# A Fourier filter with a gated convolution: the remainder of the gated input on GpSimd instead of VectorE for nine of the last ten blocks

## The chip, the cores and the metric

The kernel runs on one core of one Trainium2 chip. The metric is the device time of one execution in microseconds (us), lower is better. The core has TensorE (PE in the profile, its weight loads are PEld), VectorE (DVE), ScalarE (ACT), GpSimd (POOL) and the queue of SyncE (SP), which issues nearly all DMAs here. The engines run side by side and each works through its own instructions in order.

## The reference

```python
def _attn_ref(x, w_r, w_i, b_r, b_i):          # x: (8, 3200, 256)
    X = np.fft.rfft(x, axis=1)
    Yr = Xr @ w_r - Xi @ w_i + b_r
    Yi = Xr @ w_i + Xi @ w_r + b_i
    # soft threshold of both parts by 0.01
    y = np.fft.irfft(Yr + 1j * Yi, n=3200, axis=1)

def _moe_ref(x, w_val, conv_w, w_out):         # x is y from above
    gate_pre = sum(conv_w[k] * xp[:, k:k + S, :] for k in range(5))   # causal, per channel
    gate = 1 / (1 + np.exp(-gate_pre))
    val = x @ w_val
    return (gate * val) @ w_out                # (8, 3200, 256)
```

So each of eight batches goes through a Fourier transform, a complex channel mixing with a threshold, the inverse transform, and then a gated block: a causal convolution with five taps and a sigmoid make the gate, a 256x256 product makes the value, and the gated value is multiplied by `w_out`.

## The kernel before, in words

The transform is split into two factors (64 and 50) so that TensorE can do it with small matrices, with two passages through DRAM for each batch. The gated part of a batch is done in eight blocks of 400 positions, written (b, k) below for batch b and block k. All 64 blocks but the last, (7,7), go through the same steps:

- **positions** (L779): 128 small matmuls finish the inverse transform into `y_p` (L803), and ScalarE copies the block into `y_sb` (L810).
- **taps** (L844): for two blocks at once (for the last two blocks, (7,6) and (7,7), one at a time) ScalarE computes the first tap of each of two channel halves into an accumulator `acc` (L857), VectorE adds the other four taps, eight instructions in all (L860, called *tap steps* below, 800 elements in each partition for a pair, 400 for a single block), and ScalarE applies the sigmoid (L871).
- **value**: TensorE multiplies the block by `w_val` into `v_ps`. From block (6,7) on this is done with plain fp32 weights (L831, 4 matmuls, which the profile counts as 8), before that with high and low parts (L835, 12 matmuls).
- **product** (L902): VectorE multiplies `v_ps` in PSUM with the sigmoid in `acc` and writes the gated value back to `acc`.
- **split** (L353): ScalarE rounds the gated value to a high part (L360, the *cast*), and VectorE subtracts it from the gated value, which gives the low part (L362, the *remainder*). Both lie in `gated`.
- **output**: TensorE multiplies `gated` by the high and low parts of `w_out` into `o_ps` (L835, 12 matmuls), ScalarE copies it to `o` (L926), and SP stores it (L928). The last block (7,7) has no split: its gated value is multiplied in plain fp32 (L831).

The order of the work is made before the program is built. Every piece of work is entered into a plan with its engine, a due time, a duration in a table of costs (`dve`, `act` and the like) and the pieces it needs. `Plan.order` (L115) then goes through the plan as a list scheduler: at each step it takes the engine whose next piece can begin first, and among the pieces that can begin within a slack of that time the one that is due first. The instructions are written in that order, so each engine's queue is fixed. The buffers rotate with fixed numbers of slots: `v_ps`, `o_ps` and `y_p` share two PSUM slots (`ps_2`), `acc` has two, `gated` has two (`g_hl`) and `o` has two. The first writer of a slot waits for all readers of the tile that had it before.

GpSimd has only a few memsets at the start and two additions (L937) which make the plain fp32 weights.

The two lines that the change touches are the remainder in `split` and its call in `gated`:

```python
add(at + 0.001, "DVE", dve(n), lambda: nc.vector.tensor_tensor(out=low(), in0=src(),
    in1=f32(high()), op=ALU.subtract), [*uses, hl[0]], [hl[1]])
gs = [*split(at + own("gate", b) + 0.1, 2 * TB, kh, gate, ...
```

Of the kernel before, what the change touches and what calls it, by code (L numbers as in the profile page):

```python
# [11 lines left out]
F32R = mybir.dt.float32r  # L12
# [3 lines left out]
ALU = mybir.AluOpType  # L16

B, S, D = 8, 3200, 256
P = 128
# [9 lines left out]
TB = NH * MB * N2  # L29
# [54 lines left out]
class Plan:  # L84
# [11 lines left out]
    def add(self, at, engine, busy, fn, uses=(), sets=(), new=None, delay=None, mode="r", kb=0, chain=None, extra=0, moves=1, ways=16, ins=0):  # L96
        n = len(self.pieces)
        before = set()
        for key in uses:
            before |= set(self.writers.get(key, ()))  # L100
        for key in sets:
            before |= set(self.readers.get(key, ())) | set(self.writers.get(key, ()))
        for key in uses:
            self.readers.setdefault(key, []).append(n)
        for key in sets:
            self.writers[key], self.readers[key] = [n], []
        p = dict(n=n, at=round(at, 5), engine=engine, busy=busy, fn=fn, before=before, new=new or {}, mode=mode, kb=kb, extra=extra, moves=moves, ways=ways, ins=ins,
                 tiles={key[:2] for key in (*uses, *sets)}, delay=busy + LAND[engine] if delay is None else delay)
        p["behind"] = {self.last[chain]} if chain in self.last else set()
        if chain:  # L110
            self.last[chain] = n
        self.pieces.append(p)
        return n
# [132 lines left out]
def dve(n, copy=False):  # L246
    return 67 + n / (1.92 if copy else 0.96)


def act(n, kind="copy"):  # L250
    return {"copy": 45, "cast": 95, "mul": 104, "conv": 187, "relu": 198, "sigmoid": 103}[kind] + n / 1.2
# [42 lines left out]
         "acc": 2, "g_hl": 2, "o": 2, "ps_s2": 2, "ps_y": 1, "ps_k": 2, "ps_2": 2, "a_dram": 2, "z_dram": 2}  # L294


LATE = [(b, k) for b in (B - 2, B - 1) for k in range(NB)]


@with_exitstack  # L300
def fourier_filter_then_gated_conv(ctx: ExitStack, tc: tile.TileContext, x, w_r, w_i, b_r, b_i,
                                   w_val, conv_w, w_out, f1, f2, g1, g2, eye, out):
    nc = tc.nc
# [3 lines left out]
    dram = ctx.enter_context(tc.tile_pool(name="dram", bufs=2, space=bass.MemoryType.DRAM))  # L307
    LATE_VAL, LATE_OUT = set(LATE[int(O["late_val"]):]), set(LATE[int(O["late_out"]):])
    plan = Plan(SLOTS)
    add = plan.add  # L310
    tl = {}

    def f32(ap):
        return ap.bitcast(F32)
# [20 lines left out]
    def buffer(key, tag, shape, dtype=F32):  # L335
        if tag == "ps_k":
            tl[key] = k_bank[:, k_count[0] % 2, :]
            k_count[0] += 1
            return tl[key]
        pool = ps if tag.startswith("ps_") else dram if tag.endswith("_dram") else sb  # L340
        tl[key] = pool.tile(shape, dtype, name=key[0], tag=tag, bufs=SLOTS[tag])
        return tl[key]
# [7 lines left out]
    def two_banks(key):  # L350
        return buffer(key, "ps_2", [P, 2, 512])

    def split(at, n, key, src, high, low, uses=(), new=None, first=None):  # L353

        hl = key + ("high",), key + ("low",)

        def cast():
            if first:
                first()
            nc.scalar.copy(out=high(), in_=src())  # L360
        add(at, "ACT", act(n, "cast"), cast, uses, [hl[0]], new, chain=key[0])
        add(at + 0.001, "DVE", dve(n), lambda: nc.vector.tensor_tensor(out=low(), in0=src(), in1=f32(high()), op=ALU.subtract),  # L362
            [*uses, hl[0]], [hl[1]])
        return hl

# [409 lines left out]
    def y_at(k, c, tap=H0):  # L775
        lo = (k * MB + tap) * N2
        return y_sb[:, c, :, lo:lo + MB * N2]
# [48 lines left out]
    def matrix(key, e, w, src, whole):  # L826
        p = two_banks(key) if e == 0 else tl[key]
        n = 0
        if whole:
            for c in range(2):  # L830
                nc.tensor.matmul(p[:, e, 0:TB], w()[:, c, e * P:(e + 1) * P], src(0, c), start=c == 0, stop=c == 1)  # L831
            return
        for c in range(2):
            for hw, hy in ((0, 0), (1, 0), (0, 1)):
                nc.tensor.matmul(p[:, e, 0:TB], w[:, hw, c, e * P:(e + 1) * P], src(hy, c), start=n == 0, stop=n == 5)  # L835
                n += 1

    def blocks_at_once(b, k):
        return 1 if b == B - 1 and k >= NB - 2 else 2

    def own(name, b):
        return O[name] + O.get(f"{name}_{b}", 0.0)
# [31 lines left out]
    def gated(b, k, at):  # L874
        bk = (b, k)
        here = [("y", k, 0)]
        nb = blocks_at_once(b, k)
        k0 = k - k % nb
        ky, kv, kh, kp, ko = (("y_hl", bk), ("v_ps", bk), ("gated", bk), ("o_ps", bk), ("o", bk))
        if bk in LATE_VAL:  # L880
            vs = [*here, ("w_late", 0, 0)]
            vm = lambda e: matrix(kv, e, lambda: w_late[0], lambda h, c: y_at(k, c), True)
        else:
            src = y_sb[:, :, :, (k * MB + H0) * N2:(k * MB + H0 + MB) * N2]
            view = lambda j: tl[ky][:, j].rearrange("p c (h n) -> p c h n", h=NH)
            vs = [*split(at + own("y", b), 2 * TB, ky, lambda: src, lambda: view(0), lambda: view(1), here, {ky: "y_hl"},
                         lambda: buffer(ky, "y_hl", [P, 2, 2, TB], F32R)), ("w", "w_val", "high"), ("w", "w_val", "low")]
            vm = lambda e: matrix(kv, e, wv_sb, lambda h, c: tl[ky][:, h, c, :], False)
        if k == k0:

            vs = [*vs, *[("y", j, 0) for j in range(k + 1, k + nb)]]
        for e in range(2):
            add(at + own("val", b), "PE", 1344 if bk in LATE_VAL else 1092, lambda e=e: vm(e), vs, [kv + (e,), *([("turn", "read", (b, 2 + e))] if k == NB - 1 else [])],
                {kv: "ps_2"} if e == 0 else None, chain="val", ins=12)


        kg = ("acc", (b, k0))
        gate = lambda: tl[kg][:, :, :, (k - k0) * MB * N2:(k - k0 + 1) * MB * N2]
        hn = lambda ap: ap.rearrange("p c (h n) -> p c h n", h=NH)
        if k == k0:  # L900
            taps(b, k0, nb, at)
        add(at + own("gate", b), "DVE", dve(2 * TB), lambda: nc.vector.tensor_tensor(  # L902
            out=gate(), in0=hn(tl[kv][:, :, 0:TB]), in1=gate(), op=ALU.mult), [kv + (0,), kv + (1,), kg + (0,), kg + (1,)], [kg + ("gated", k)])
        if bk in LATE_OUT:
            gs = [kg + ("gated", k), ("w_late", 0, 0)]
            om = lambda e: matrix(kp, e, lambda: w_late[1], lambda h, c: gate()[:, c], True)
        else:
            gs = [*split(at + own("gate", b) + 0.1, 2 * TB, kh, gate, lambda: hn(tl[kh][:, 0]), lambda: hn(tl[kh][:, 1]),
                         [kg + ("gated", k)], {kh: "g_hl"}, lambda: buffer(kh, "g_hl", [P, 2, 2, TB], F32R)),
                  ("w", "w_out", "high"), ("w", "w_out", "low")]  # L910
            om = lambda e: matrix(kp, e, wo_sb, lambda h, c: tl[kh][:, h, c, :], False)
        for e in range(2):
            add(at + own("project", b), "PE", 1344 if bk in LATE_OUT else 1092, lambda e=e: om(e), gs, [kp + (e,)],
                {kp: "ps_2"} if e == 0 else None, ins=12)
        dst = out[b].rearrange("(c p) n -> p c n", p=P)[:, :, k * TB:(k + 1) * TB]
        kind = at + own("project", b) + 0.1
        if bk == (B - 1, NB - 1):
            def keep(e):
                o = buffer(ko, "o", [P, 2, TB]) if e == 0 else tl[ko]
                (nc.scalar.copy, nc.vector.tensor_copy)[e](out=o[:, e], in_=tl[kp][:, e, 0:TB])  # L920
            for e, eng in enumerate(("ACT", "DVE")):
                add(kind, eng, act(TB) if e == 0 else dve(TB), lambda e=e: keep(e), [kp + (e,)], [ko + (e,)],
                    {ko: "o"} if e == 0 else None)
                add(kind, "SP", 400, lambda e=e: nc.sync.dma_start(out=dst[:, e], in_=tl[ko][:, e]), [ko + (e,)], (), kb=200)
            return
        add(kind, "ACT", act(2 * TB), lambda: nc.scalar.copy(out=buffer(ko, "o", [P, 2, TB]), in_=tl[kp][:, :, 0:TB]),  # L926
            [kp + (0,), kp + (1,)], [ko + (0,)], {ko: "o"})
        add(kind, "SP", 400, lambda: nc.sync.dma_start(out=dst, in_=tl[ko]), [ko + (0,)], (), kb=400)  # L928
# [102 lines left out]
```

## Time and profile before

| what | value |
|---|---|
| time, median of 3 runs | 879.93 us (878.89 to 881.42) |
| profiled execution, its own time | 881.59 us |
| span of the profiled execution | 879.8 us, granted TensorE clock 0.994 on average |
| busy: PE, DVE, ACT, POOL | 857.8, 759.1, 604.9, 3.8 us |
| remainders of the gated input (L362, `gated`), from 690 us on | 21, together 20.6 us |
| tap steps of the last batch begin | 823.90 us |
| last product ends | 872.63 us (starts at 871.64, takes 0.99) |
| last block's output product on PE | starts at 872.91 us |

A row of the timeline gives the start, the time it took, the engine, the line, the operation and the tiles written and read, with their partitions and elements; in brackets stands how long the engine was idle before it, and what ended the idle time. Consecutive instructions of one engine overlap a little in the profile, so the time that one takes out of an engine is the distance of two starts. In groups and sources, three numbers with slashes are the shortest, median and longest duration in ns.

### The profile page before, as it was taken

How to read it: one execution, taken by the hardware profiler on the slowest of the kernel's cores; microseconds unless marked ns; L12 is line 12 of the kernel's file. 1: busy time of each engine (PE TensorE's matmuls, PEld its weight loads, DVE VectorE, ACT ScalarE, POOL GpSimd, SP SyncE). 2: the span in 40 equal slices, each digit the busy share in tenths (PEclk: the TensorE clock that was granted, in tenths of full speed). 3: DMA queues.
4: the chain of work that ended last, by engine and by line, in shares of the span. 5: the costliest groups of instructions: out<-in, count | busy, mean ns of one | idle time of the engine just before them, and what ended most of it. 6: DMA issues, size and time to landing. Idle time of an engine off the chain costs nothing.

```text
span 879.8 us, 24544 instructions
## 1 busy us (share of the span) xinstructions
PE 857.8 (97%) x10400; PEld 745.5 (85%) x10400; DVE 759.1 (86%) x1143; ACT 604.9 (69%) x928; POOL 3.8 (0%) x11
## 2 busy tenths in 40 slices
PE   7999999999999999999999999999999999998997
PEld 3778788878999898898899889898899999998775
DVE  2346888999989996999879997899969999899796
ACT  2456666977677766877667776877658775875664
POOL 0000000000000000000000000000100000000000
PEclk9999999999999999999999999999999999999999
DMA  6878886786554476565855576646746353423522
GB/s 212 253 244 253 240 269 197 265 251 199 165 184 146 148 218 212 177 185 172 272 168 171 175 237 205 218 122 208 244 133 202 104 171 94 142 103 110 186 76 94
DMA packets 105289, 163.34 MB, mean 186 GB/s; under 512 B 9690, under 2 KB 78172, under 8 KB 105180
## 3 DMA queue, kind: packets, MB, share of 16 engines
q1 hardware_dynamic: 103764, 158.43, 58.1%
q10 hardware_dynamic: 1416, 3.34, 1.2%
q8 instruction: 82, 1.34, 0.6%
q14 instruction: 27, 0.22, 0.1%
HBM read 82.05 MB, written 79.69 MB: 184 GB/s over the span
## 4 chain that ended last, share of the span: by engine, by line
PE 78%; DVE 15%; DMA 3%; ACT 2%; issue 1%; SPq 0%; ACTq 0%; DVEq 0%
PE y_ps L704 14%; PE o_ps L835 12%; PE v_ps L835 11%; PE s L634 9%; PE z_ps L747 8%; PE k_bank L709 7%; PE y_p L803 6%; DVE acc L860 6%; PE p L583 5%; DMA x<-in_x 2%; PE warm L951 1%; DVE acc L902 1%; PE v_ps L831 1%; DMA f_sb<-in_f 1%; DVE gated L362 1%
## 5 line engine op out<-in xcount | busy, mean ns | idle before, releaser
L860 DVE SCALAR_TENSOR_TENSOR acc<-y_sb,cw_sb,acc 128x800 f32<-128x800 f32 (+1 forms) x264 | 258.7, 1017 | 11.4 <-ACT acc L857 11.2
L704 PE MATMUL y_ps<-w_sb,xs 128*128 128x256 f32 x1152 | 157.7, 286 | 0.7 <-DVE yb L718 0.7
L835 PE MATMUL o_ps<-gated,wo_sb 128*128 128x400 f32 x756 | 153.5, 352 | 0.0
L704 PEld LDWEIGHTS y_ps<-w_sb,xs 128*128 128x128 f32 x1152 | 144.3, 190 | 8.6 <-issue 3.9
L835 PEld LDWEIGHTS o_ps<-gated,wo_sb 128*128 128x128 f32 x756 | 135.6, 189 | 3.4 <-issue 1.0
L835 PE MATMUL v_ps<-y_hl,wv_sb 128*128 128x400 f32 x660 | 130.6, 346 | 1.1 <-ACT y_sb L810 1.1
L634 PEld LDWEIGHTS s<-f_sb,a 128*128 128x128 f32 x800 | 100.3, 191 | 24.9 <-issue 19.0
L835 PEld LDWEIGHTS v_ps<-y_hl,wv_sb 128*128 128x128 f32 x660 | 118.7, 188 | 2.1 <-ACT y_sb L810 1.3
L634 PE MATMUL s<-f_sb,a 128*128 128x128 f32 x800 | 111.9, 280 | 1.3 <-DVE xs L692 1.2
L747 PE MATMUL z_ps<-tp,g_sb 64*64 64x256 f32 x1536 | 93.7, 380 | 0.0
L688 ACT CAST xs<-s 128x512 fp32r<-128x512 f32 x96 | 56.2, 586 | 43.0 <-PE y_ps L704 28.1
L709 PE MATMUL k_bank<-w_sb,xs 128*128 128x256 f32 x576 | 85.3, 283 | 0.4 <-DVE yb L715 0.4
L722 ACT ACTIVATE tp<-yb,nlam 128x512 f32<-128x512 f32 (+1 forms) x104 | 73.6, 708 | 16.5 <-DVE yb L718 9.0
L718 DVE TENSOR_TENSOR yb<-y_ps,yb 128x512 f32<-128x512 f32 x96 | 65.4, 681 | 19.9 <-PE y_ps L704 19.7
L747 PEld LDWEIGHTS z_ps<-tp,g_sb 64*64 64x64 f32 x1536 | 57.1, 133 | 27.1 <-issue 5.8
L360 ACT CAST gated<-acc 128x800 fp32r<-128x800 f32 x63 | 54.2, 861 | 37.1 <-DVE acc L902 33.5
L709 PEld LDWEIGHTS k_bank<-w_sb,xs 128*128 128x128 f32 x576 | 74.8, 188 | 5.1 <-issue 1.1
L926 ACT COPY o<-o_ps 128x800 f32<-128x800 f32 x63 | 51.9, 823 | 38.0 <-PE o_ps L835 37.8
L803 PEld LDWEIGHTS y_p<-g_sb,zl 50*64 50x64 f32 x4096 | 66.1, 135 | 13.9 <-issue 5.1
L902 DVE TENSOR_TENSOR acc<-v_ps,acc 128x800 f32<-128x800 f32 x64 | 62.9, 983 | 16.9 <-PE v_ps L835 14.1
L724 DVE SCALAR_TENSOR_TENSOR tp<-yb,tp 128x512 f32<-128x512 f32 (+1 forms) x104 | 68.8, 661 | 7.7 <-ACT tp L722 7.4
L803 PE MATMUL y_p<-g_sb,zl 50*64 50x50 f32 x4096 | 71.8, 220 | 3.4 <-issue 2.2
(80 smaller groups left out, 1028.4 us busy)
## 6 DMA issues: line engine op xcount, KB each, us to landing
zl<-z_dram SPq DMA_DIRECT2D x128, 200.0 KB
out<-o SPq DMA_DIRECT2D x63, 400.0 KB
a_dram<-s SPq DMA_DIRECT2D x120, 208.0 KB
a<-a_dram SPq DMA_DIRECT2D x96, 256.0 KB
z_dram<-z_t SPq DMA_DIRECT2D x48, 512.0 KB
x<-in_x SPq DMA_DIRECT2D x120, 200.0 KB
a_dram<-s ACTq DMA_DIRECT2D x8, 208.0 KB
x<-in_x ACTq DMA_DIRECT2D x8, 200.0 KB
```

The source lines that it names most:

```text
L634: nc.tensor.matmul(spec()[:, c, :, i, :], tl[ka][:, i0 + i, c * P:(c + 1) * P], f2_of(i), start=True, stop=True)
L688: nc.scalar.copy(out=tl[kx][:, 0:512], in_=tl[k2].rearrange("p a b -> p (a b)"))
L704: nc.tensor.matmul(p[:, 1 - r, :], xm(hx, c, r), w_sb[:, m, hw, c, :], start=k == 0, stop=k == 5)
L709: nc.tensor.matmul(p, sm(hx, c), w_sb[:, 0, hw, c, :], start=k == 0, stop=k == 5)
L718: add(at + 0.2, "DVE", dve(2 * D), lambda: nc.vector.tensor_tensor(out=yb(), in0=tl[ky], in1=yb(), op=ALU.add), [ky + (0,)], [kb + (0,)])
L722: nc.scalar.activation(out=buffer(kt, "tp", [P, 2, D])[:, 0:n], in_=tl[kb][:, 0:n], func=AF.Relu, bias=nlam)
L724: add(at + 0.2, "DVE", dve(n * D), lambda: nc.vector.scalar_tensor_tensor(out=tl[kt][:, 0:n], in0=tl[kb][:, 0:n], scalar=LAM, in1=tl[kt][: ...
L747: nc.tensor.matmul(p[e * HP:(e + 1) * HP, i, j * D:(j + 1) * D], g[i * HP:(i + 1) * HP, r, e * HP:(e + 1) * HP], tl[kts[j]][i * HP:(i + 1) ...
L803: nc.tensor.matmul(pv[h][e * HP:(e + 1) * HP, c, m, :], zt[half(h), m, c * P + e * HP:c * P + (e + 1) * HP], g2_sb[half(h), :], start=True ...
L835: nc.tensor.matmul(p[:, e, 0:TB], w[:, hw, c, e * P:(e + 1) * P], src(hy, c), start=n == 0, stop=n == 5)
L860: nc.vector.scalar_tensor_tensor(out=acc(c), in0=y_of(c, j), scalar=cw_sb[:, c, j:j + 1], in1=acc(c), op0=ALU.mult, op1=ALU.add)
L902: add(at + own("gate", b), "DVE", dve(2 * TB), lambda: nc.vector.tensor_tensor(out=gate(), in0=hn(tl[kv][:, :, 0:TB]), in1=gate(), op=ALU. ...
```

## The change

The remainder (the subtraction that gives the low part) is issued on GpSimd for blocks (6,6), (6,7) and (7,0) to (7,6). The last block, (7,7), has no remainder. In the plan it is entered for engine POOL with a cost of 2.7 ns for each of 800 elements instead of `dve(800)`. Operands and tiles are the same. The 54 earlier remainders of the gated input stay on VectorE, and so do all those of `y_hl`.

```diff
+POOL_LOW = 2.7
 LATE = [(b, k) for b in (B - 2, B - 1) for k in range(NB)]
...
-    def split(at, n, key, src, high, low, uses=(), new=None, first=None):
+    def split(at, n, key, src, high, low, uses=(), new=None, first=None, pool=False):
...
         add(at, "ACT", act(n, "cast"), cast, uses, [hl[0]], new, chain=key[0])
-        add(at + 0.001, "DVE", dve(n), lambda: nc.vector.tensor_tensor(out=low(), in0=src(), in1=f32(high()), op=ALU.subtract),
+        eng, busy = ("POOL", POOL_LOW * n) if pool else ("DVE", dve(n))
+        add(at + 0.001, eng, busy, lambda: (nc.gpsimd if pool else nc.vector).tensor_tensor(out=low(), in0=src(), in1=f32(high()), op=ALU.subtract),
             [*uses, hl[0]], [hl[1]])
...
             gs = [*split(at + own("gate", b) + 0.1, 2 * TB, kh, gate, lambda: hn(tl[kh][:, 0]), lambda: hn(tl[kh][:, 1]),
-                         [kg + ("gated", k)], {kh: "g_hl"}, lambda: buffer(kh, "g_hl", [P, 2, 2, TB], F32R)),
+                         [kg + ("gated", k)], {kh: "g_hl"}, lambda: buffer(kh, "g_hl", [P, 2, 2, TB], F32R), pool=bk >= (B - 2, 6)),
```

Since the plan is made with the new engine and cost, the order of other pieces changes too, but only from the product of block (6,7) on; ahead of it every engine's queue is as before. Up to the first function the line numbers of the changed kernel are 1 higher, behind `split` 2 higher: the tap steps are L862 there, the products L904, the remainder L364, the value and output products L833 and L837.

The first place is VectorE in the middle of the last batch, from the first tap step of that batch. `acc_10622` is the accumulator of blocks (7,0) and (7,1); `acc_10745` before and `acc_10740` now is that of (7,2) and (7,3); `acc_10879` before and `acc_10907` now is that of (7,4) and (7,5). Before:

```order
L860 SCALAR_TENSOR_TENSOR acc_10622<-y_sb_78,cw_sb_76,acc_10622 128x800 x8
L362 TENSOR_TENSOR gated_10639<-acc_10359,gated_10639 128x800
L902 TENSOR_TENSOR acc_10622<-v_ps_10727,acc_10622 128x4x200
L860 SCALAR_TENSOR_TENSOR acc_10745<-y_sb_78,cw_sb_76,acc_10745 128x800
L902 TENSOR_TENSOR acc_10622<-v_ps_10740,acc_10622 128x4x200
L362 TENSOR_TENSOR gated_10759<-acc_10622,gated_10759 128x800
L860 SCALAR_TENSOR_TENSOR acc_10745<-y_sb_78,cw_sb_76,acc_10745 128x800
L362 TENSOR_TENSOR gated_10803<-acc_10622,gated_10803 128x800
L860 SCALAR_TENSOR_TENSOR acc_10745<-y_sb_78,cw_sb_76,acc_10745 128x800 x6
L860 SCALAR_TENSOR_TENSOR acc_10879<-y_sb_78,cw_sb_76,acc_10879 128x800 x2
L902 TENSOR_TENSOR acc_10745<-v_ps_10899,acc_10745 128x4x200
```

Now:

```order
L862 SCALAR_TENSOR_TENSOR acc_10622<-y_sb_78,cw_sb_76,acc_10622 128x800 x8
L862 SCALAR_TENSOR_TENSOR acc_10740<-y_sb_78,cw_sb_76,acc_10740 128x800 x3
L904 TENSOR_TENSOR acc_10622<-v_ps_10751,acc_10622 128x4x200
L862 SCALAR_TENSOR_TENSOR acc_10740<-y_sb_78,cw_sb_76,acc_10740 128x800 x5
L904 TENSOR_TENSOR acc_10622<-v_ps_10872,acc_10622 128x4x200
L904 TENSOR_TENSOR acc_10740<-v_ps_10899,acc_10740 128x4x200
L862 SCALAR_TENSOR_TENSOR acc_10907<-y_sb_78,cw_sb_76,acc_10907 128x800 x5
L904 TENSOR_TENSOR acc_10740<-v_ps_10928,acc_10740 128x4x200
L862 SCALAR_TENSOR_TENSOR acc_10907<-y_sb_78,cw_sb_76,acc_10907 128x800 x3
L904 TENSOR_TENSOR acc_10907<-v_ps_10957,acc_10907 128x4x200
```

The remainders are gone from VectorE's queue, the tap steps of (7,2) and (7,3) have moved ahead of the products of (7,0) and (7,1), and the products of (7,1) and (7,2) now stand next to each other, where eleven instructions lay between them before.

The second place is TensorE at the same point, in the changed kernel: `v_ps_10872`, `v_ps_10899` and `v_ps_10928` are the values of (7,1), (7,2) and (7,3), and the `o_ps` rows are the outputs of (7,0) and (7,1).

```order
L833 MATMUL v_ps_10872<-y_sb_78,w_late_8659 128x400 x4
L837 MATMUL o_ps_10882<-gated_10833,wo_sb_74 128x400 x12
L833 MATMUL v_ps_10899<-y_sb_78,w_late_8659 128x400 x4
L837 MATMUL o_ps_10909<-gated_10896,wo_sb_74 128x400 x12
L833 MATMUL v_ps_10928<-y_sb_78,w_late_8659 128x400 x4
```

The three tiles `v_ps_10872`, `o_ps_10882` and `v_ps_10899` are taken in this order from the two slots of `ps_2`, so the third has the slot of the first. Before, the values of (7,0) and (7,1) stood together ahead of the output of (6,7).

The third place is GpSimd behind the two additions, in the changed kernel (before, nothing stands there): the nine remainders in the order of the blocks.

```order
L364 TENSOR_TENSOR gated_10498<-acc_10359,gated_10498 128x800
L364 TENSOR_TENSOR gated_10639<-acc_10359,gated_10639 128x800
L364 TENSOR_TENSOR gated_10833<-acc_10622,gated_10833 128x800
L364 TENSOR_TENSOR gated_10896<-acc_10622,gated_10896 128x800
L364 TENSOR_TENSOR gated_10925<-acc_10740,gated_10925 128x800
L364 TENSOR_TENSOR gated_10955<-acc_10740,gated_10955 128x800
L364 TENSOR_TENSOR gated_10980<-acc_10907,gated_10980 128x800
L364 TENSOR_TENSOR gated_11004<-acc_10907,gated_11004 128x800
L364 TENSOR_TENSOR gated_11043<-acc_10973,gated_11043 128x800
```

The last place is VectorE's end, in the changed kernel: `acc_10907` is the pair (7,4), (7,5), `acc_10973` is block (7,6) and `acc_11025` is block (7,7).

```order
L904 TENSOR_TENSOR acc_10907<-v_ps_10957,acc_10907 128x4x200
L862 SCALAR_TENSOR_TENSOR acc_10973<-y_sb_78,cw_sb_76,acc_10973 128x400 x2
L904 TENSOR_TENSOR acc_10907<-v_ps_10969,acc_10907 128x4x200
L862 SCALAR_TENSOR_TENSOR acc_10973<-y_sb_78,cw_sb_76,acc_10973 128x400 x6
L904 TENSOR_TENSOR acc_10973<-v_ps_11000,acc_10973 128x800
L862 SCALAR_TENSOR_TENSOR acc_11025<-y_sb_78,cw_sb_76,acc_11025 128x400 x8
L904 TENSOR_TENSOR acc_11025<-v_ps_11059,acc_11025 128x800
L922 COPY o_11093<-o_ps_11085 128x400
```

Before, the same tap steps and products stood here with four remainders between them. The order of the stores on SP is unchanged.

## The prediction

> **What bounds the kernel now.** First the page: TensorE is busy nearly throughout, VectorE next.
>
> ```profile
> span 879.8 us, 24544 instructions
> PE 857.8 (97%) x10400; PEld 745.5 (85%) x10400; DVE 759.1 (86%) x1143; ACT 604.9 (69%) x928; POOL 3.8 (0%) x11
> ```
>
> The change lies in the last 60 us, so I read that part of the chain of waits (start, us, what):
>
> ```profile
> 823.90 7.79 DVE acc L860 x8
> ...
> 857.23 0.91 DVE acc L902
> 858.15 0.04 issue
> 858.19 2.95 PE v_ps L831 x8
> ...
> 870.89 2.19 PE o_ps L835 x12
> ...
> 873.15 0.83 ACT o L926
> ```
>
> From 823.90 to 858 the chain runs almost wholly on VectorE, behind it on TensorE. So VectorE looks like the place to save. VectorE's groups between 823.85 and 873 (count, busy us, mean ns, idle before), and the rows in which it waits inside that stretch:
>
> ```profile
> L860 DVE SCALAR_TENSOR_TENSOR acc<-y_sb,cw_sb,acc 128x800 f32<-128x800 f32 (+1 forms) x40 | 33.0, 877 | 4.3 <-ACT acc L857 4.2
> L902 DVE TENSOR_TENSOR acc<-v_ps,acc 128x800 f32<-128x800 f32 x8 | 7.9, 986 | 0.6 <-ACT acc L871 0.6
> L362 DVE TENSOR_TENSOR gated<-acc,gated 128x800 fp32r<-128x800 f32 x8 | 7.9, 984 | 0.4 <-ACT gated L360 0.4
> ...
> 863.10 0.99 DVE L362 TENSOR_TENSOR gated<-acc,gated 128x800 fp32r<-128x800 f32 x1 [0.39 <-ACT gated L360]
> 864.78 1.72 DVE L860 SCALAR_TENSOR_TENSOR acc<-y_sb,cw_sb,acc 128x400 f32<-128x400 f32 x3 [0.69 <-ACT acc L857]
> 871.64 0.99 DVE L902 TENSOR_TENSOR acc<-v_ps,acc 128x800 f32<-128x800 f32 x1 [0.60 <-ACT acc L871]
> ```
>
> VectorE waits 0.39 + 0.69 + 0.60 = 1.7 us in 48.7 us: it is full. But so is TensorE:
>
> ```profile
> 840.78 2.46 PE L835 MATMUL o_ps<-gated,wo_sb 128*128 128x400 f32 x12
> 843.08 2.85 PE L831 MATMUL v_ps<-y_sb,w_late 128*128 128x400 f32 x8
> ...
> 858.19 2.95 PE L831 MATMUL v_ps<-y_sb,w_late 128*128 128x400 f32 x8 [0.39 <-DVE acc L902]
> 860.67 2.66 PE L835 MATMUL o_ps<-gated,wo_sb 128*128 128x400 f32 x12
> 863.17 2.85 PE L831 MATMUL v_ps<-y_sb,w_late 128*128 128x400 f32 x8
> 865.55 2.66 PE L835 MATMUL o_ps<-gated,wo_sb 128*128 128x400 f32 x12
> ...
> 872.91 2.85 PE L831 MATMUL o_ps<-acc,w_late 128*128 128x400 f32 x8
> ```
>
> An output and a value together take 865.55 - 860.67 = 4.88 us from start to start, and from 840.78 to the last matmuls at 872.91 TensorE waits once, 0.39 us. The last product ends at 871.64 + 0.99 = 872.63, 0.28 us before the last matmuls that need it. The two engines finish together: work taken from VectorE gains next to nothing, work added to VectorE costs nearly its full length.
>
> **The change, part by part.**
>
> *Removed from VectorE.* Eight of the nine remainders lie behind 823.90. One costs the distance of two starts:
>
> ```profile
> 848.90 0.98 DVE L362 TENSOR_TENSOR gated<-acc,gated 128x800 fp32r<-128x800 f32 x1
> 849.80 1.04 DVE L860 SCALAR_TENSOR_TENSOR acc<-y_sb,cw_sb,acc 128x800 f32<-128x800 f32 x1
> ```
>
> 849.80 - 848.90 = 0.90 us; 8 x 0.90 = **-7.2 us**. The ninth, of (6,6), gives nothing, since VectorE idles behind it:
>
> ```profile
> 818.58 0.98 DVE L362 TENSOR_TENSOR gated<-acc,gated 128x800 fp32r<-128x800 f32 x1
> 823.90 7.79 DVE L860 SCALAR_TENSOR_TENSOR acc<-y_sb,cw_sb,acc 128x800 f32<-128x800 f32 x8 [3.55 <-ACT acc L857]
> ```
>
> *Added on GpSimd, price d of one.* The nearest rows are the two additions of the same kind, 512 elements wide, with VectorE's rows at the same time:
>
> ```profile
> 634.91 1.28 POOL L937 TENSOR_TENSOR w_late<-wv_sb 128x512 f32<-128x512 f32 x1 [633.18 <-PE p L583]
> 636.13 1.46 POOL L937 TENSOR_TENSOR w_late<-wo_sb 128x512 f32<-128x512 f32 x1
> ...
> 634.72 0.68 DVE L692 TENSOR_TENSOR xs<-s,xs 128x512 fp32r<-128x512 f32 x1
> 635.32 1.15 DVE L696 TENSOR_TENSOR xs<-sx,xs 128x256 fp32r<-128x256 f32 x1
> 636.39 0.68 DVE L718 TENSOR_TENSOR yb<-y_ps,yb 128x512 f32<-128x512 f32 x1
> 636.99 0.41 DVE L691 TENSOR_TENSOR sx<-s,sx 128x256 f32<-128x256 f32 x1
> ...
> L696 DVE TENSOR_TENSOR xs<-sx,xs x96: 406/414/1148, 40.0 to 772.6; 128x256 fp32r<-128x256 f32 x96
> ```
>
> The second overlaps L696 until 635.32 + 1.15 = 636.47, that is 0.34 us; without these it took 1.12. Scaled by 800/512: 1.28 gives 2.0, 1.12 gives 1.75; I take d = 1.9. Lower bound 1.7 (1.12 with 0.1 us of it fixed, as in the 98 ns memset below), upper bound 2.3 (1.46 scaled whole).
>
> ```profile
> L952 POOL MEMSET nlam<- 128x1 f32 x1 | 0.1, 98 | 0.3 <-POOLq L1016 0.3
> ```
>
> *What GpSimd does to VectorE.* The same rows show the price that the diff hides. L696 reads two tiles in SBUF, and the one of its 96 executions that met a GpSimd addition took 1148 ns, where the median is 414; it ended 0.28 us after the addition did (634.91 + 1.28 = 636.19), about the time that it needs by itself. It stood still until GpSimd was done. L692, L718 and L691 read one tile in PSUM and one in SBUF, ran in the same 2.7 us, and took their usual 0.68 and 0.41. So VectorE with two SBUF inputs and GpSimd with two SBUF inputs exclude each other. A tap step reads `y_sb` and `acc`, both SBUF; a product reads PSUM, and is free.
>
> The Trainium skill says the same as a general rule (SBUF — State Buffer, "SBUF: two separate sides"): VectorE and GpSimd share a port pair as an exclusive lock for a whole instruction, a VectorE operation with two SBUF inputs needs it against a GpSimd operation that reads SBUF, and whichever starts first keeps it. The trace agrees in its one case (1148 against 414 ns); that a tap step behaves like L696 no run here shows. Its figure for a GpSimd addition of 2048 fp32 elements is 4497 ns (GPSIMD Engine Reference, "Elementwise — side-by-side cycle accounting"), an estimate of 1.76 us for 800 elements; with it the term below would be 11.4 in place of 12.4, and the time 886.6.
>
> Now along the new order, remainder by remainder. (6,7) follows its cast, which ran at 824.61, in the middle of the first eight tap steps: VectorE stands for d. (7,0) and (7,2) are each followed on VectorE by five tap steps, (7,3) by three, (7,5) by six, (7,6) by eight: d each. Behind the product of (7,4) stand two short tap steps (1.1 us) and then a product: the remainder begins after the cast (0.85), so the product's 0.90 hides part: d - 0.9. (7,1) meets the new wait below, 0. Together 7d - 0.9 = **+12.4 us**.
>
> ```profile
> 823.76 0.95 ACT L857 ACTIVATE acc<-y_sb,cw_sb 128x800 f32<-128x800 f32 x1
> 824.61 0.85 ACT L360 CAST gated<-acc 128x800 fp32r<-128x800 f32 x1
> ...
> 867.33 1.17 DVE L860 SCALAR_TENSOR_TENSOR acc<-y_sb,cw_sb,acc 128x400 f32<-128x400 f32 x2
> ```
>
> *Moved.* The product of (7,2) now follows that of (7,1) directly on VectorE. On TensorE the value of (7,2) takes the PSUM slot of the value of (7,1), so it begins only when that product is done, and the next product waits for its whole length: **+2.8 us** of idle VectorE (2.85 in the row at 843.08). Behind that product queue the tap steps of (7,4), which also need ScalarE's first tap, and that needs `acc` back from GpSimd: 0.85 + 1.9 + 0.95 = 3.7 after the product of (7,1), against 2.8 + 0.98 on VectorE. So this is just covered, and a longer d would show here too. The other products that follow their own tap steps ((7,4), (7,6), (7,7)) wait some 0.6 each for the sigmoid, as at 871.64: 1.8, in place of the 1.7 that VectorE waits now, 0. Stores and loads keep their order on SP, 0.
>
> *Sum* for the last product: -7.2 + 12.4 + 2.8 = +8.0, less the 0.28 lead: +7.7 us. The profiled execution took 881.59 (span 879.8 and 1.8 around it) and would take 889.3; it lies 1.66 above the median of the runs, so I predict 879.93 + 7.7 = **887.6 us**. With d = 1.7 it is 886.2; with d = 2.3, where (7,1) outlasts its cover by 0.4, 890.8.
>
> **The rivals.**
>
> *No exclusion for tap steps.* For it: L696 is one execution of another form. Against it: nothing else explains 1148 ns once in 96. Then VectorE has 7.2 - 2.8 = 4.4 us of slack, and TensorE sets the end. It can gain no more than its waits behind 822 us, 0.39 and the two below, 1.3 us in all; half of them gives 879.3, not slower.
>
> ```profile
> 838.20 1.73 PE L803 MATMUL y_p<-g_sb,zl 50*64 50x50 f32 x103 [0.59 <-ACT o L926]
> 840.25 0.60 PE L803 MATMUL y_p<-g_sb,zl 50*64 50x50 f32 x25 [0.32 <-issue]
> ```
>
> *VectorE wins the port.* Where tap steps follow back to back, GpSimd may have to wait for the end of the row of them. For it: eight tap steps of 1.04 us take 7.79, so each begins before the last has ended, and the port may never look free. Against it: at 636.13 L696, which waited, was served before GpSimd's second instruction; the turns changed. Then the remainder of (6,7) begins at 831.7 instead of 825.5 and ends at 833.6. TensorE, which now has this output ahead of the value of (7,0), stands from 828.7 to 833.6; less the 1.3 us of waits that this swallows, +3.6. At the end the remainder of (7,6) follows the last tap step: d + 2.2 for its output ahead of the last matmuls, against 0.6 + 0.99 for the last product, +2.5. Together 886.0.
>
> ```profile
> 828.70 5.64 PE L831 MATMUL v_ps<-y_sb,w_late 128*128 128x400 f32 x16
> ```
>
> *GpSimd is slower than scaled.* The gated block is a strided view and the output another type (fp32r), which no GpSimd row shows. At d = 3.0: 7d - 0.9 = 20.1, and 1.1 for (7,1): 896.1.
>
> That the change does not do what it says is out: GpSimd's queue holds the nine remainders.
>
> **How the numbers follow.** Forecast 0.75, VectorE first 0.12, slow GpSimd 0.06, no exclusion 0.06, anything else 0.01. One thing raises every slower case: where TensorE waited 2.9 us before 804, its granted clock in that stage fell,
>
> ```profile
> 800.00:810.00 10.00, 7.07 (x48) 6.28 (x41) 9.74 (x11) 5.09 (x7) 0.00 (x0) 0.83 0.27 98
> ```
>
> 0.17 of 10 us, so 1.7 us are lost if a new wait does the same. 890.8 and 1.7 give the upper end, 892.5; two of the six full blocks falling into waits (-3.8) the lower, 883.8. Less than 0.3% (2.6 us) can't be told from no change here. Slower 0.93 (all but no exclusion and the rest), the same 0.05, faster 0.02.
>
> **What would show it.** Tap steps of 1.04 us that take 2 to 3 us, one for each of six or seven remainders, and products that stay at 0.98; GpSimd rows of 1.7 to 2.3 us, or up to 0.9 more where they had to wait for the port; a VectorE wait of 2.8 us on `v_ps` ahead of the product of (7,2); a chain that stays on VectorE to the last product, with TensorE waiting behind 858. Wrong would be: tap steps at 1.04 next to a running remainder (no exclusion), remainders that begin only with a product (VectorE first), or rows of 3 us.

## The result, and the profile after

The changed kernel takes 891.8 us (median of 4 runs, 891.19 to 893.31) against 879.84 us before: a ratio of 1.0124 with a 95% interval of 1.0098 to 1.015. It is slower by 12 us by the medians, by 10.9 us (8.6 to 13.2) by the ratio, where 7.7 were predicted, and lies inside the predicted range. The profiled execution took 892.22 us, 0.42 above its median, with a span of 890.4; that of before took 881.59, 1.75 above its median. The two profiles therefore show 10.6 us of the 12.

The page of the changed kernel:

```profile
span 890.4 us, 24551 instructions
PE 862.1 (97%) x10400; PEld 747.4 (84%) x10400; DVE 762.2 (86%) x1134; ACT 605.9 (68%) x928; POOL 23.9 (3%) x20
```

VectorE has nine instructions fewer and is busy 3.1 us longer. To the first tap step of the last batch the two executions are alike (823.90 before, 824.04 now); everything that follows is new. The chain of waits from there (start, us, what):

```profile
824.04 10.47 DVE acc L862 x10
...
836.37 0.91 DVE acc L904
...
837.32 3.49 PE y_p L805 x126
840.81 4.89 PE v_ps L833 x8
...
845.72 1.00 DVE acc L904
...
847.75 1.89 POOL gated L364
...
849.66 0.97 ACT acc L859
...
850.65 0.99 DVE acc L904
851.64 6.42 DVE acc L862 x5
...
874.79 3.78 PE o_ps L837 x12
```

Where the chain before stayed on VectorE to 858 and then ran on TensorE, it now leaves VectorE at 837 and at 846, comes back to it each time, and ends on TensorE only from 874.79. The steps over GpSimd and ScalarE from 847.75 on are what came last by the profile ahead of the product of (7,2) at 850.65. But the value of (7,2) on TensorE ended within 0.1 us of them, and in the memset kernel below, in which ScalarE is done with this step about 1 us earlier, the same two products are as far apart (4.94 us from start to start, 4.93 here). So the value sets that start.

VectorE's groups from 818 us on show both halves of the loss (count, busy us, mean ns, idle before; one of the nine products lies ahead of the last batch):

```profile
L862 DVE SCALAR_TENSOR_TENSOR acc<-y_sb,cw_sb,acc 128x800 f32<-128x800 f32 (+1 forms) x40 | 43.0, 1141 | 3.1 <-ACT acc L859 3.1
L904 DVE TENSOR_TENSOR acc<-v_ps,acc 128x800 f32<-128x800 f32 x9 | 8.9, 988 | 8.4 <-ACT acc L859 3.9 <-PE v_ps L833 2.9 <-ACT acc L873 1.5
```

The same forty tap steps cost 43.0 us instead of 33.0, and the products, which waited 0.6 us before, now wait 8.4. The products themselves are as long as ever.

**The tap steps.** The five behind the product of (7,0), by their shortest, median and longest duration in ns:

```profile
L862 DVE SCALAR_TENSOR_TENSOR acc<-y_sb,cw_sb,acc x5: 1039/1041/2668, 837.2 to 842.7; 128x800 f32<-128x800 f32 x5
```

The timeline has the GpSimd row that met them, and a place further on where a product and then two short tap steps meet a remainder:

```profile
838.30 2.63 POOL L364 TENSOR_TENSOR gated<-acc,gated 128x800 fp32r<-128x800 f32 x1 [10.49 <-ACT gated L361]
...
866.41 0.98 DVE L904 TENSOR_TENSOR acc<-v_ps,acc 128x800 f32<-128x800 f32 x1
866.44 1.91 POOL L364 TENSOR_TENSOR gated<-acc,gated 128x800 fp32r<-128x800 f32 x1 [3.82 <-ACT gated L361]
867.31 2.02 DVE L862 SCALAR_TENSOR_TENSOR acc<-y_sb,cw_sb,acc 128x400 f32<-128x400 f32 x2
```

One of the five tap steps took 2668 ns, 1.63 us more than the others. GpSimd's row is 2.63 long, since it first waited some 0.75 for the tap step that was running; undisturbed it takes 1.88 to 1.91. At 866.41 the product, with one input in PSUM, runs its 0.98 us right through a remainder, and the tap steps behind it take 2.02 instead of 1.17. The Trainium skill's rule (SBUF — State Buffer, "SBUF: two separate sides") asks for two SBUF inputs on VectorE's side, or a two-port mode, and the trace agrees for these two: 2668 ns with two SBUF inputs, 0.98 us as ever with one.

**TensorE.** Its rows in the timeline around the first two places, and its last two:

```profile
837.32 3.49 PE L805 MATMUL y_p<-g_sb,zl 50*64 50x50 f32 x128 [1.02 <-DVE acc L904]
840.74 4.94 PE L833 MATMUL v_ps<-y_sb,w_late 128*128 128x400 f32 x8
845.22 2.64 PE L837 MATMUL o_ps<-gated,wo_sb 128*128 128x400 f32 x12
847.69 2.85 PE L833 MATMUL v_ps<-y_sb,w_late 128*128 128x400 f32 x8
...
881.03 2.64 PE L837 MATMUL o_ps<-gated,wo_sb 128*128 128x400 f32 x12
883.51 2.85 PE L833 MATMUL o_ps<-acc,w_late 128*128 128x400 f32 x8
```

And three stretches of 10 us, in which the third number from the end is the granted clock:

```profile
830.00:840.00 10.00, 7.83 (x191) 6.09 (x189) 10.00 (x11) 6.49 (x8) 1.70 (x1) 0.90 0.39 126
840.00:850.00 10.00, 10.00 (x47) 6.67 (x45) 4.69 (x4) 4.59 (x6) 2.81 (x2) 0.76 0.04 15
870.00:880.00 10.00, 7.99 (x31) 6.70 (x30) 9.40 (x12) 4.52 (x7) 3.37 (x2) 0.83 0.23 84
```

The value of (7,1) took 4.94 us instead of 2.85, because the granted clock fell there (0.50 from 838 to 844 us, 1.00 again from 845) and once more in the stretch from 870. The product of (7,1) waited 2.0 us for it, the last one 0.87.

So the stretch from the first tap step of the last batch to the end of the last product grew from 48.73 us (823.90 to 872.63) to 58.56 (824.04 to 882.60), by 9.8. Rows overlap a little, so I count by the distance of starts. The eight remainders take 7.4 us of the old stretch, the products 7.5 of the old and 7.4 of the new, the waits 1.68 and 8.36; that leaves 32.2 us for the tap steps before and 42.8 now. So: remainders gone -7.4, tap steps +10.6, the wait ahead of the product of (7,2) +3.9, waits for values of a slowed TensorE +2.9, the other waits -0.1 (0.94 + 0.60 in place of 1.68). To rounding, these make the 9.8. The rest of the 10.6 is 0.14 ahead of the stretch and 0.63 behind it: the last block's matmuls start 0.91 us behind the last product (883.51 against 882.60), where it was 0.28, since TensorE is until then in the output of (7,6).

### The profile page after: what moved, and what is told of

The parts are those of the page before. It is cut to its first block, busy times and chain, and to the rows that moved or that the text cites. A ratio compares the mean times of both kernels' runs of the same rounds, so it can differ in the third digit from the quotient of the medians.

```text
span 890.4 us, 24551 instructions
## 1 busy us (share of the span) xinstructions
PE 862.1 (97%) x10400; PEld 747.4 (84%) x10400; DVE 762.2 (86%) x1134; ACT 605.9 (68%) x928; POOL 23.9 (3%) x20
## 4 chain that ended last, share of the span: by engine, by line
PE 76%; DVE 17%; DMA 3%; ACT 2%; issue 2%; SPq 0%; POOL 0%; ACTq 0%; DVEq 0%; POOLq 0%
PE y_ps L706 14%; PE o_ps L837 12%; PE v_ps L837 11%; PE s L636 9%; PE z_ps L749 8%; DVE acc L862 7%; PE k_bank L711 7%; PE y_p L805 7%; PE p L585 5%; DVE acc L904 2%; DMA x<-in_x 1%; PE warm L953 1%; DMA f_sb<-in_f 1%; DVE yb L717 1%; DVE y_hl L364 1%
## 5 line engine op out<-in xcount | busy, mean ns | idle before, releaser
L862 DVE SCALAR_TENSOR_TENSOR acc<-y_sb,cw_sb,acc 128x800 f32<-128x800 f32 (+1 forms) x264 | 269.3, 1060 | 9.9 <-ACT acc L859 9.7
L837 PE MATMUL o_ps<-gated,wo_sb 128*128 128x400 f32 x756 | 153.5, 352 | 3.2 <-DVE acc L904 2.8
L837 PEld LDWEIGHTS o_ps<-gated,wo_sb 128*128 128x128 f32 x756 | 135.5, 189 | 7.0 <-DVE acc L904 3.8
L837 PE MATMUL v_ps<-y_hl,wv_sb 128*128 128x400 f32 x660 | 130.7, 346 | 1.1 <-ACT y_sb L812 1.1
L837 PEld LDWEIGHTS v_ps<-y_hl,wv_sb 128*128 128x128 f32 x660 | 118.7, 188 | 2.2 <-ACT y_sb L812 1.3
L904 DVE TENSOR_TENSOR acc<-v_ps,acc 128x800 f32<-128x800 f32 x64 | 63.1, 986 | 24.3 <-PE v_ps L837 13.6
L720 DVE TENSOR_TENSOR yb<-y_ps,yb 128x512 f32<-128x512 f32 x96 | 65.6, 684 | 20.3 <-PE y_ps L706 20.1
```

Of the source, the lines that this page charges most:

```text
L720: add(at + 0.2, "DVE", dve(2 * D), lambda: nc.vector.tensor_tensor(out=yb(), in0=tl[ky], in1=yb(), op=ALU.add), [ky + (0,)], [kb + (0,)])
L862: nc.vector.scalar_tensor_tensor(out=acc(c), in0=y_of(c, j), scalar=cw_sb[:, c, j:j + 1], in1=acc(c), op0=ALU.mult, op1=ALU.add)
```

## The experiments

Theory P is that of the prediction: VectorE's tap steps, with two inputs in SBUF, stand still while GpSimd reads SBUF, and VectorE has no room for it. Its rivals: O, the loss comes from the new order; C, a good part comes from TensorE's lower clock; W, any GpSimd instruction holds VectorE up. The kernels of the first four were run together, and the last three together, each with runs of the kernel before on the same chip. Beside the time I give the length of the same stretch (first tap step of the last batch to the end of the last product) in the profile, since what lies ahead of it varies from execution to execution; it is one execution of each kernel. The last column is the busy time of the forty tap steps, as in the groups above.

| kernel | ratio to before (95% interval) | stretch, us | tap steps, us |
|---|---|---|---|
| before | | 48.73 | 33.0 |
| the change | 1.0124 (1.0098 to 1.015) | 58.56 | 43.0 |
| memset in place of the subtraction | 1.0000 (0.9977 to 1.0024) | 48.21 | 32.4 |
| new order, subtraction on VectorE | 1.0045 (1.0021 to 1.0070) | 52.36 | 32.9 |
| old order, subtraction on GpSimd | 1.0057 (1.0033 to 1.0081) | 55.88 | 43.9 |
| the change, TensorE's gaps filled | 1.0086 (1.0060 to 1.0112) | 56.22 | 43.1 |
| one input read | one run, 886.09 us | 53.71 | 36.5 |
| subtraction twice | one run, 898.05 us | 68.28 | 53.0 |
| old order, memset | 0.9995 (0.9974 to 1.0015) | 47.57 | 32.7 |

### GpSimd without reading

```diff
-        add(at + 0.001, eng, busy, lambda: (nc.gpsimd if pool else nc.vector).tensor_tensor(...),
+        def rest():
+            if pool:
+                nc.gpsimd.memset(f32(low()), 0.0)
+            else:
+                nc.vector.tensor_tensor(out=low(), in0=src(), in1=f32(high()), op=ALU.subtract)
+        add(at + 0.001, eng, busy, rest,
```

> The changed kernel with a GpSimd memset of the low part in place of each of the nine subtractions: the order on every engine is that of the changed kernel, GpSimd still writes the same tile at the same place, but reads nothing from SBUF. The computation leaves out the low part of the gated input in these nine blocks. Theory P (a tap step with its two SBUF inputs stands still while GpSimd reads SBUF): no tap step longer than 1.05 us in the last batch, VectorE's tap steps there back from 43.0 to 33.0 us, and the time falls by about 10 us to 880 to 883, where TensorE sets the end again. Theory O (the new order costs it: products that stand next to each other, later values): tap steps don't matter, 889 to 892. Theory W (any GpSimd instruction, a writing one too, holds VectorE up): tap steps longer by the memset's own length of some 0.8 us, 884 to 887.

Measured: no difference from before, ratio 1.0000. The first eleven tap steps of the batch (shortest, median, longest):

```profile
L867 DVE SCALAR_TENSOR_TENSOR acc<-y_sb,cw_sb,acc x11: 1044/1048/1051, 822.5 to 832.2; 128x800 f32<-128x800 f32 x11
```

Two of the memsets that ran beside them, in the timeline:

```profile
823.21 0.77 POOL L366 MEMSET gated<- 128x800 f32 x1 [10.97 <-PE o_ps L842]
825.47 0.77 POOL L366 MEMSET gated<- 128x800 f32 x1 [1.49 <-PE o_ps L842]
```

Not one is longer than 1051 ns. A GpSimd instruction that only writes costs VectorE nothing: W is out, and with the same order and without the reads the whole loss is gone, so O alone is out too. But the new wait is there, and longer than predicted. The timeline at the products of (7,1) and (7,2), first VectorE, then TensorE:

```profile
840.43 0.99 DVE L909 TENSOR_TENSOR acc<-v_ps,acc 128x800 f32<-128x800 f32 x1 [1.51 <-PE v_ps L838]
845.37 0.99 DVE L909 TENSOR_TENSOR acc<-v_ps,acc 128x800 f32<-128x800 f32 x1 [3.95 <-PE v_ps L838]
...
839.92 2.66 PE L842 MATMUL o_ps<-gated,wo_sb 128*128 128x400 f32 x12
842.42 2.85 PE L838 MATMUL v_ps<-y_sb,w_late 128*128 128x400 f32 x8
```

The first product ends at 841.42, but TensorE is still in the output of (7,0), which stands in its queue ahead of the value of (7,2), until 842.42. Only then come the 2.85 us. VectorE waits 3.95, and it costs nothing that shows here, because VectorE is without its remainders.

### The new order alone

```diff
-        add(at + 0.001, eng, busy, lambda: (nc.gpsimd if pool else nc.vector).tensor_tensor(...),
+        add(at + 0.001, eng, busy, lambda: nc.vector.tensor_tensor(...),
```

> The plan of the changed kernel, with its order for all other pieces, but the nine subtractions are issued on VectorE at the place in time where the plan put them. Theory P: no exclusion, VectorE has its work of before (8 x 0.90 us more than the changed kernel without blocking) and the wait between the products of (7,1) and (7,2) of 2.8 us, of which a remainder of 0.9 fills a part: 881 to 883. Theory O: the order alone costs it, 888 to 892. Theory C (TensorE's clock falls after its new waits): half clock here too if the order makes the waits, 884 to 886.

Measured: 1.0045, which is 4.0 us (1.9 to 6.2), above what P gave (881 to 883, the median is 886.6) and below O (888 to 892). Tap steps are at their old length. VectorE has all its work of before, and waits 5.5 us in the stretch where it waited 1.7. P had counted only the wait between the two products, of which the remainder of (7,1) fills 0.9; the one ahead of (7,1), and three for sigmoids (0.94, 0.61 and 0.60), come on top. The timeline of the first two:

```profile
841.00 0.99 DVE L904 TENSOR_TENSOR acc<-v_ps,acc 128x800 f32<-128x800 f32 x1 [0.47 <-PE v_ps L833]
842.91 0.99 DVE L364 TENSOR_TENSOR gated<-acc,gated 128x800 fp32r<-128x800 f32 x1 [0.93 <-ACT gated L361]
845.85 0.99 DVE L904 TENSOR_TENSOR acc<-v_ps,acc 128x800 f32<-128x800 f32 x1 [1.94 <-PE v_ps L833]
```

The granted clock was 1.00 from 810 to 880, so C has no part in these 4 us. The order costs them when VectorE is full, and nothing that shows when it isn't.

### The old order with GpSimd

```diff
-        eng, busy = ("POOL", POOL_LOW * n) if pool else ("DVE", dve(n))
+        eng, busy = "DVE", dve(n)
```

> The nine subtractions on GpSimd, but entered into the plan as VectorE work of before's cost, so all engines keep the order of the kernel before, with the remainders cut out of VectorE's queue. Theory P: seven or eight remainders block VectorE by 1.6 us each (12 us) and 7.2 us are gone, without the 2.8 us wait between two products: 884 to 887, tap steps of 2.6 us next to each remainder. Theory O: without the new order the loss is gone, 879 to 881.

Measured: 1.0057, 5.0 us (2.9 to 7.1), as P had it. VectorE's groups have the tap steps as long as in the change:

```profile
L862 DVE SCALAR_TENSOR_TENSOR acc<-y_sb,cw_sb,acc 128x800 f32<-128x800 f32 (+1 forms) x40 | 43.9, 1159 | 6.3 <-ACT acc L859 6.3
```

And in the timeline a wait appears that the old order did not have: the first tap of (7,7) on ScalarE needs the accumulator that GpSimd is still reading for (7,5).

```profile
870.33 1.88 POOL L364 TENSOR_TENSOR gated<-acc,gated 128x800 fp32r<-128x800 f32 x1 [2.37 <-ACT gated L361]
872.90 1.73 DVE L862 SCALAR_TENSOR_TENSOR acc<-y_sb,cw_sb,acc 128x400 f32<-128x400 f32 x3 [3.06 <-ACT acc L859]
```

Its profiled execution was the slowest of its runs, with a granted clock of 0.83 in the stretches from 820 and from 840, so its stretch is on the long side.

### TensorE's gaps filled

```diff
+    def fill(n):
+        for _ in range(n):
+            nc.tensor.matmul(k_bank[:, 0, :], eye_sb, f2_sb[:, 0:2 * P], start=True, stop=True)
+
+    FILL = {("v_ps", (7, 0)): 2, ("y_p", (7, 4)): 2, ("o_ps", (7, 2)): 2, ("o_ps", (7, 4)): 4}
```

`fill` is called behind the matmuls of these four tiles; nobody reads `k_bank` there.

> The changed kernel with matmuls that nobody reads put into TensorE's queue where it waited: two 128x256 fp32 behind the value of (7,0), two behind the positions of (7,4), two behind the output of (7,2), four behind the output of (7,4), each 0.43 us at full clock, less than the wait there. All else is as in the changed kernel. Theory C (part of the loss is TensorE at half the granted clock between 836 and 843 and between 874 and 877): the granted clock stays at 1.0 to the end, the value of (7,1) takes 2.85 instead of 4.94 us, the wait of the product of (7,1) (2.0 us) goes and that of the last product (0.87): 888 to 890. Rival (VectorE's blocked time alone sets the end): 891 to 893, the clock makes no difference to the end.

Measured: 889.1 us, 1.0086. The granted clock stayed at 1.00 where it had fallen:

```profile
840.00:850.00 10.00, 10.00 (x42) 7.56 (x41) 6.07 (x8) 6.93 (x8) 3.02 (x2) 1.00 0.11 41
870.00:880.00 10.00, 9.43 (x40) 6.95 (x39) 7.93 (x10) 5.26 (x8) 2.30 (x1) 1.00 0.22 82
```

The product of (7,1) no longer waits, while the tap steps are those of the change (43.1 us) and the wait for (7,2) stays. The last product waits 0.61 us for its sigmoid, as it did before the change, so of the 0.87 only 0.26 is gone. The last matmuls follow it at once:

```profile
841.91 0.98 DVE L915 TENSOR_TENSOR acc<-v_ps,acc 128x800 f32<-128x800 f32 x1
846.83 0.99 DVE L915 TENSOR_TENSOR acc<-v_ps,acc 128x800 f32<-128x800 f32 x1 [3.93 <-ACT acc L870]
877.54 0.99 DVE L915 TENSOR_TENSOR acc<-v_ps,acc 128x800 f32<-128x800 f32 x1 [0.61 <-ACT acc L884]
...
878.59 2.95 PE L840 MATMUL o_ps<-acc,w_late 128*128 128x400 f32 x8 [0.28 <-DVE acc L915]
```

The stretch is 2.3 us shorter than the change's, and behind it the last matmuls start 0.06 us after the last product, not 0.91. So in these two executions C is right about 2.3 us of the 9.8, and about 0.85 us more between the last product and the last matmuls. (That more matmuls make the kernel faster is not shown by the times: the change was run on another chip, and the two intervals overlap.) The profile puts the wait at 846.83 down to ScalarE; by the case without reading it is the value of (7,2), which ends within 0.1 us of it.

### One input instead of two

```diff
-        (subtraction on GpSimd)
+                nc.gpsimd.tensor_copy(out=low(), in_=src())
```

> The changed kernel with a GpSimd copy of the gated input into the low part in place of each subtraction: one tensor read from SBUF instead of two, written to the same place, the order unchanged. The computation uses the whole gated input as the low part in these blocks. Theory P1 (any GpSimd read of SBUF holds up a tap step): next to each copy one tap step takes the copy's length less about 0.25 us longer than its 1.04, as with the subtractions (2.67 for a subtraction of 1.88). Theory P2 (only two inputs against two inputs): tap steps of 1.04 everywhere. The copy should take between the 0.77 us of the memset and the 1.88 of the subtraction, so by P1 the last batch's tap steps sum to 37 to 42 us, by P2 to 33.

Measured: the copy takes 0.85 us undisturbed, and the five tap steps behind the product of (7,0) take 5.48 us (timeline):

```profile
835.13 5.48 DVE L867 SCALAR_TENSOR_TENSOR acc<-y_sb,cw_sb,acc 128x800 f32<-128x800 f32 x5
835.34 1.54 POOL L366 CAST gated<-acc 128x800 fp32r<-128x800 f32 x1 [10.54 <-DVE acc L909]
816.64 0.85 POOL L366 CAST gated<-acc 128x800 fp32r<-128x800 f32 x1 [179.88 <-DVE acc L909]
```

The same group without reads (behind the product of (7,0) in the memset kernel) took 4.90. So a copy that reads one tensor holds a tap step up for 0.58 us, 0.27 less than its own 0.85; a subtraction of 1.88 does so for 1.63, 0.25 less. P1 holds: one read on GpSimd's side is enough. The sum of 36.5 us is just below the 37 to 42 that were expected, since the copy is nearer to the memset than I thought. In its stretch TensorE was slowed too (granted clock 0.78 from 840 to 850), and the product of (7,1) waited 3.81 us for its value.

### The subtraction twice

```diff
+            for _ in range(2 if pool else 1):
                 (nc.gpsimd if pool else nc.vector).tensor_tensor(...)
```

> The changed kernel with each of the nine GpSimd subtractions issued twice in a row, the order unchanged. Theory P: the blocked time doubles. Tap steps grow by 1.63 us for each subtraction that meets them, so their sum goes from 43.0 to 53 to 56 us, with two long tap steps of about 2.7 us for each block where VectorE takes its turn between the two, or one of 4.5 where it does not; the second of (7,1) now also lengthens the wait ahead of the tap steps of (7,4). Time 902 to 908. If the loss came from the order and TensorE's clock alone, it would stay at 889 to 893.

Measured: 898.05 us in its one run, below the 902 to 908 that were expected, though far above 893. The tap steps come to 53.0 us, the lower end of what was expected, and the stretch is 9.7 us longer than the change's. The miss in the time lies outside it: it began at 820.90, 3.1 us earlier than in the change's execution, and what lies behind it took 0.8 us less. In the timeline, those behind the products of (7,0) and (7,3):

```profile
835.69 8.13 DVE L865 SCALAR_TENSOR_TENSOR acc<-y_sb,cw_sb,acc 128x800 f32<-128x800 f32 x5
860.07 4.59 DVE L865 SCALAR_TENSOR_TENSOR acc<-y_sb,cw_sb,acc 128x800 f32<-128x800 f32 x3
```

Five tap steps took 8.13, against 6.52 with one subtraction and 4.90 with none: 1.6 us for each. The three behind the product of (7,3) stayed at 4.59: the second subtraction came behind the last of them and fell into a wait. The growth of 10.0 us is about what six second subtractions cost. The second of (7,1) lengthened the wait ahead of the tap steps of (7,4), as expected, by 0.91 us.

### The ceiling in the old order

```diff
-        eng, busy = ("POOL", POOL_LOW * n) if pool else ("DVE", dve(n))
+        eng, busy = "DVE", dve(n)
...
+                nc.gpsimd.memset(f32(low()), 0.0)
```

> The ceiling: the order of the kernel before on all engines, the nine remainders taken off VectorE, and a GpSimd memset of the low part in their place, which reads nothing (the low part of the gated input is left out of the computation in these blocks). If VectorE was what ended last from 823.9 to 858, as the chain of waits has it, 7.2 us less on it should show as several us: 873 to 877. If TensorE is as full as VectorE there, as the prediction's first part has it, no more than its waits of 1.3 us can be gained: 878.5 to 880, no difference that can be told.

Measured: 0.9995, no difference. VectorE, without its remainders, waits for TensorE now:

```profile
842.64 0.99 DVE L909 TENSOR_TENSOR acc<-v_ps,acc 128x800 f32<-128x800 f32 x1 [1.73 <-PE v_ps L838]
847.43 0.99 DVE L909 TENSOR_TENSOR acc<-v_ps,acc 128x800 f32<-128x800 f32 x1 [0.91 <-PE v_ps L838]
```

The stretch became 1.2 us shorter, but the last matmuls then started 0.93 us behind its end instead of 0.28, so only 0.5 us of it reached them. TensorE's 1.3 us of waits shrank to 0.64. With remainders that take nothing from VectorE, this is about the most that taking them off it can bring in this order, and it can't be told from nothing.

## Why the prediction was right, and where its sizes were off

**What bounds the kernel: right.** The step "work taken from VectorE gains next to nothing, work added costs nearly its full length" is what the two memset kernels (1.0000 and 0.9995) and the subtraction on GpSimd in the old order (1.0057) show. The chain of waits alone, with VectorE from 823.9 to 858, would have said the opposite.

**The price of one remainder: right.** d was taken as 1.9; undisturbed rows are 1.88 to 1.91. The other rows, up to 2.63, hold a wait for the tap step that was running and not more work.

**The exclusion: right, a little oversized.** It was read from one instruction of 96, and the tap steps behaved like it. The term was 7d - 0.9 = 12.4; the tap steps grew by 10.6, by the distance of starts as well as by rows against the memset kernel, which has the same order (43.0 against 32.4). The prediction took the whole length d out of VectorE for each of six remainders; a tap step stands for 1.63 us and not for 1.9, which is 1.6 of the 1.8 us. The short tap steps behind (7,4) took 0.85 more, where d - 0.9 gave 1.0.

**The moved product: mechanism right, size off.** The term was 2.8, measured 3.9. The step that failed is "it begins only when that product is done": TensorE had also to finish the output of (7,0), which stands between the two values and takes 2.47 us, while the product takes 0.99. What was to cover the remainder of (7,1) did: ScalarE's first tap of (7,4) ended at 850.63, as the product of (7,2) began.

**The clock: left out of the sum.** It stood in the prediction only as a reason for the upper end, with 1.7 us. It cost 2.3 us of the stretch, by the filled kernel. With it, and with -7.4, 10.6 and 3.9 in place of -7.2, 12.4 and 2.8, the prediction's sum is -7.4 + 10.6 + 3.9 + 2.3 = 9.4 of the 9.8 measured in the stretch; the waits for sigmoids, counted as 1.8 in place of 1.7, came to 2.15 (0.94 + 0.60 + 0.61). The clock also undid the last term, "less the 0.28 lead": in the filled kernel the lead is used up but for 0.06 us, in the change it grew to 0.91. For the same reason one sign failed: the chain did not stay on VectorE to the last product but ended on TensorE from 874.79; in the filled kernel it stays there from 846.83 on, but for sigmoids. That the measured time lies inside the range rests partly on one term too large against others too small.

**The rivals.** "No exclusion" fell with the first long tap step. "VectorE wins the port" would have begun the remainder of (6,7) at 831.7:

```profile
825.68 2.13 POOL L364 TENSOR_TENSOR gated<-acc,gated 128x800 fp32r<-128x800 f32 x1 [5.30 <-ACT gated L361]
```

It began at 825.68 and waited about 0.25 us for one tap step; no remainder waited for more than one. "GpSimd is slower than scaled" fell with the rows of 1.88. (By the prediction's own terms its time is 896.4, not 896.1: 20.1 + 1.1 is 8.8 more than 12.4. Nothing hangs on it.) What was expected of (6,6), nothing, held.

What stays open: 1.3 us of the 12 lie in the spread of the executions, not in the two profiles; and how often TensorE's clock falls in an execution of the change is not known, since one of them has a profile.

## What to carry to other kernels

An instruction moved to GpSimd is not gone from VectorE if both read SBUF: price it as its length on GpSimd, less some 0.25 us, taken out of whatever VectorE instruction with two inputs in SBUF runs beside it, and let VectorE work there on PSUM, or idle. Before work is taken off the engine on which the chain of waits lies, count the idle time of the other engine in the same stretch: here TensorE's 1.3 us was the most there was to gain. When a plan is remade with new costs, look for neighbours in a queue that each need the same slot, and count everything that stands between them on the other engine.

## What the runs showed of the hardware that was not expected

- A tap step is held up for less than GpSimd's row is long, by 0.25 us for the subtraction (1.88 against 1.63) and 0.27 for the copy (0.85 against 0.58).
- A plain VectorE copy from SBUF to SBUF, with one input, stood still too: L818 took 0.95 us next to the remainder of (6,6), against 0.37 in the same place before. In the three other kernels that ran the subtraction there it took 0.75 to 0.80, and 0.37 in the four that had none beside it. The Trainium skill (SBUF — State Buffer, "SBUF: two separate sides") counts VectorE's copies in a two-port mode among the instructions that need the shared ports; the trace agrees so far, and which mode L818 ran in no row tells.

```profile
819.66 0.95 DVE L818 COPY y_sb<-y_sb 128x400 f32<-128x400 f32 x1 [1.18 <-ACT y_sb L812]
818.50 1.89 POOL L364 TENSOR_TENSOR gated<-acc,gated 128x800 fp32r<-128x800 f32 x1 [179.49 <-ACT gated L361]
```

- TensorE's clock fell without a long wait, and the waits alone don't tell when it falls. In the change TensorE waited 1.14 and 1.02 us on either side of 64 small matmuls (64x50) ahead of the drop at 838; in the memset kernel, where the waits at this place were 0.62 and 1.01 us, the clock stayed at 1.00. But with the copy on GpSimd, where these waits were 0 and 1.02 us and the next 0.87, it fell to 0.50 by 838; and with the subtractions on VectorE it stayed at 1.00 through 0.40, 1.02 and 0.88. Nor does a long wait always bring it down: from 800 to 810 us the granted clock was 0.83 before, with a wait of 2.93 us, and 1.00 in the change, with one of 2.95 us ahead of the same matmuls. The Trainium skill puts the drop behind an idle window of about 3.4 us (TensorE: Matmul & The Clock Gate, "Part 1: The HAM clock gate (the "warmup" mystery)"); here it fell around waits a third as long, and what decided it no run shows.
